# Windowed attention and two MLPs on one core: first six attention rounds on PSUM banks of their own and ahead of the weight conversions

## The chip, the core and the metric

The kernel runs on one core of a Trainium2 chip. Times are device microseconds of that core: the median of several runs, and beside it one execution that the hardware profiler recorded. TensorE (PE in the profile) multiplies matrices, VectorE (DVE), ScalarE (ACT) and GpSimd (POOL) work elementwise, SyncE (SP) issues the transfers. Each engine works through its own queue in order; semaphores tie the queues together.

## The reference, cut to what matters

```
scores = scale * q @ k.T                # 4 batches, 8 heads, 576 x 64 each
mask:  heads 0-3: 0 <= i - j < 32       # "plain"
       heads 4-7: 0 <= i - j < 128 and (i - j) % 4 == 0   # "dilated"
attn = softmax(masked scores);  x = attn @ v      # -> x: 2304 x 512
h = x @ w_in;  g = max(0.01 * h, h);  x2 = g @ w_out       # 512 -> 2048 -> 512
a = x2 @ w1;  b = x2 @ w2;  out = (a * b @ w3) @ w_out2    # 512 -> 1024 -> 512
```

The weights come as float64.

## The kernel before

**Attention** is done in 32 rounds. A round is one pair of heads and either the first 320 or the last 256 tokens of a batch. For round n: `scores(n)` (L316) multiplies qT and kT into a PSUM bank, VectorE adds the mask (L336) and takes the maximum (L338), ScalarE does the exponential (L341); `normalize(n)` (L346) makes the reciprocal on VectorE and multiplies on GpSimd (L354); `transpose_p(n)` (L360) turns the probabilities on TensorE into two PSUM tiles `ps_p` of up to three blocks each (L370), which ScalarE copies to `pT` (L372); `values(n)` (L375) multiplies them with v into `ps_o`, ScalarE writes the high part of the tile `x` (L419) and VectorE the low part (L421). `transpose_qk(m)` (L288) turns q and k of a pair of heads on TensorE (L306), and VectorE copies them to qT and kT (L309, L311). All these PSUM tiles come from one pair of banks, tag "side"; there are two more pairs, tag "h" (`bank`) and tag "acc" (`bank2`, two tiles of two banks each).

**The MLPs** run with float32 split in a high and a low part, three matmuls for each product (`mm3`, L110, lines L112 to L114). The first MLP takes a run of tokens c (320 or 256) and goes through blocks f of 128 hidden columns: `hidden(c, f)` makes `ps_h`, ScalarE applies the slope (L472), VectorE and GpSimd split it into `gs`, and two blocks later `project` adds it to `ps_x`. Run c = 0 goes through blocks 0 to 7 first, then c = 1 through all 16, then c = 0 through 8 to 15, then the others.

**Weights.** Before a block f can be used, a block of w_in and one of w_out must be converted from float64: 32 jobs, numbered by pairs (job 2f is w_in, 2f+1 is w_out). Each is a load of 512 KB into a buffer `raw` (mostly one of eight in the pool `woB`), a scaling on GpSimd (L103), two ScalarE instructions into `r` (L143, L145), a shift (L146) and a join (L147) on VectorE, called shift and join below, and then the split: a high cast (L107) and a low part (L108), on engines that the letters in `MLP_CONV` name. One letter triple stands for a job in turn: the scaling's engine, the high cast's, the low part's (A ScalarE, D VectorE, G GpSimd).

**Order.** The start is written out as a string (L700): digits load q and k, a to d load v, F loads a weight, X starts rounds 0 and 1, A is two of the four steps of an attention round, C is one conversion. Twelve A are the first six rounds. After the string the loop over blocks does, for each block ("turn"), the hidden part, some conversions (`owed_w`), some attention steps (`pace`) and the lagged projection. A scheduler then places the instructions of each engine: what stands ahead in the program has precedence, what stands behind may fill gaps. SP's own order is kept as written while weights are still converted.

Of the kernel before, what the change touches and what calls it, by code (L numbers as in the profile page):

```python
# [28 lines left out]
def tile_window_attention_two_mlps(  # L29
# [17 lines left out]
    T, DM = out.shape  # L47
# [17 lines left out]
    HP = H // 2  # L65
# [19 lines left out]
    def bank2(name):  # L85
        return psum.tile([P, 2, 512], F32, tag="acc", name=name, bufs=2)

    def side_bank(name):
        return psum.tile([P, 512], F32, tag="side", name=name, bufs=2)
# [59 lines left out]

    engine_of = {"A": nc.scalar, "D": nc.vector, "G": nc.gpsimd}  # L150
    FOLD_CONV = ("GAD", "GAG")
    MLP_CONV = ("GAD", "GDD", "GAD", "GDG")
    LAST_CONV = ("GAD",)

    class Convert:
# [70 lines left out]
    def pair(pi):  # L226
        b, h0 = divmod(pi, HP)
        return b, 2 * h0, 2 * h0 < H // 2

    def load_qk(m):  # L230
        if m >= 2 * NPAIR:
            return
        pi, nm = seq[m // 2], "qk"[m % 2]
        b, h0, plain = pair(pi)
        c = 6 if plain else 8
        n = S // c
        if m < 2 * HP:
            t = win_p.tile([P, 8, 2, D], F32, tag="win", name=f"{nm}{pi}", bufs=NF)
        else:
            t = att.tile([P, 8, 2, D], F32, tag="nat", name=f"{nm}{pi}", bufs=2)  # L240
        src = q if nm == "q" else k
        o = (b * H + h0) * S * D
        for j in range(2):
            nc.sync.dma_start(
                t[:n, :c, j, :], rows(src, o + j * S * D, [[c * D, n], [D, c], [1, D]])
            )
        nat_t[nm, pi] = t
# [40 lines left out]
    def transpose_qk(m):  # L288

        if m >= 2 * NPAIR:  # L290
            return
        pi, nm = seq[m // 2], "qk"[m % 2]
        plain = pair(pi)[2]
        c = 6 if plain else 8
        n = S // c
        t = nat_t.pop((nm, pi))
        dst = att.tile([P, S], F32, tag=nm + "T", name=f"{nm}T{pi}", bufs=2)
        if plain:
            to = dst.rearrange("d (p g c) -> d g c p", g=2, p=n)
        else:  # L300
            to = dst.rearrange("d (c p g) -> d g c p", g=2, p=n)
        for g in range(2):
            ps = side_bank(f"ps_{nm}T{pi}_{g}")
            for c1 in range(c // 2):
                src = t[:n, g * (c // 2) + c1].rearrange("p j d -> p (j d)")
                nc.tensor.transpose(ps[:, c1 * n : (c1 + 1) * n], src, ident[:n, :n])  # L306
            src = ps[:, : S // 2].rearrange("d (c p) -> d c p", p=n)
            if nm == "q":
                nc.vector.tensor_scalar(to[:, g], src, SCALE, None, op0=ALU.mult)  # L309
            else:  # L310
                nc.vector.tensor_copy(to[:, g], src)  # L311
        qk_t[nm, pi] = dst
# [47 lines left out]
    def transpose_p(n):  # L360
        s, _ = sm.pop(n)
        nb = s.shape[1]
        t = att.tile([KB, NQ, P], F32, tag="pT", name=f"pT{n}", bufs=2)[:, :nb]
        groups = [(i0, min(i0 + GROUP, nb)) for i0 in range(0, nb, GROUP)]
        pss = []
        for g, (i0, i1) in enumerate(groups):
            ps = side_bank(f"ps_p{n}_{g}")
            pss.append(ps[:KB, : (i1 - i0) * P].rearrange("k (i p) -> k i p", p=P))
            for i in range(i0, i1):
                nc.tensor.transpose(pss[g][:, i - i0], s[:, i], ident)  # L370
        for ps, (i0, i1) in zip(pss, groups):
            nc.scalar.copy(t[:, i0:i1], ps)  # L372
        pt[n] = t
# [51 lines left out]
    N_EARLY = 6  # L425
# [213 lines left out]
    with ExitStack():  # L639
# [44 lines left out]
        def kr(prefix):  # L684
            return lambda i: rawp.tile([P, 512], I32, tag="kr", name=f"{prefix}{i}", bufs=KR)

        jobs = []
        for f in range(NF):
# [4 lines left out]
            )  # L693
        conv = Convert(jobs, raw_early, kr("w"), kr("r"), MLP_CONV)

        with tc.manual_schedule(engines={mybir.EngineType.SP}):


            first = attention(0, N_EARLY)
            for x in "0aM1bFF2cFF3dFFXACAACACAACACAACACAACAC":  # L700
                if x in "0123":
                    load_qk(2 * int(x))
                    load_qk(2 * int(x) + 1)
                elif x in "abcd":
                    load_v("abcd".index(x))
                elif x == "M":
                    build_masks()
                elif x == "X":
                    transpose_qk(0)
                    transpose_qk(1)  # L710
                    scores(0)
                    scores(1)
                    transpose_qk(2)
                    normalize(0)
                    transpose_qk(3)
                elif x == "A":
                    step(first, first)
                elif x == "F":
                    conv.fetch()
                else:  # L720
                    conv.step()
            step(*[first] * 10)
# [6 lines left out]
        def mlp1(c, f, f0, f1):  # L729
            hidden(c, f)  # L730
            todo.append((c, f, f0, f1))

        def lagged():
            if len(todo) > LAG:
                project(*todo.pop(0))
# [18 lines left out]
        owed, owed_w = [0.0], [0.0]  # L754

        def pace(c):

            if xs_b[0] is None:
                owed[0] += 1.25 if turn < 8 else 0.25
            else:  # L760
                owed[0] += 2 if c < 2 else 1.5
            while owed[0] >= 1:
                owed[0] -= 1
                step(stream)
# [3 lines left out]
        turn = -1  # L768
        sp = ExitStack()
        for c, f0, f1 in runs:  # L770
# [38 lines left out]
            for f in range(f0, f1):  # L809
                turn += 1  # L810
                sp.close()
                if xs_b[0] is None:
                    sp.enter_context(tc.manual_schedule(engines={mybir.EngineType.SP}))
                mlp1(c, f, f0, f1)
                if xs_b[0] is None:
                    owed_w[0] += 1.5
                    while owed_w[0] >= 1:
                        owed_w[0] -= 1
                        conv.step()
                    if conv.made == len(conv.jobs) and not conv.done:  # L820
                        raw_es.close()
                        xsB_es, xs_b[0] = pool("xsB", "left")
                if c < C_LATE:
                    pace(c)
                elif c < NCH - 1:
                    fold_step()
                lagged()
                if c == NCH - 1:
                    conv.step()
                    if 2 <= f < 2 + NI:  # L830
                        load_wp(f - 2)
                    if 3 <= f < 3 + NI:
                        split_wp(f - 3)
                    if 11 <= f < 11 + NC:
                        split_y(0, f - 11)
                    if f == 11 + NC - 1:
                        load_y(1)
# [54 lines left out]
```

## Time and profile before

| | |
|---|---|
| median of 3 runs | 933.92 us (929.98 to 934.81) |
| profiled execution | 930.62 us, span 928.8 us |
| TensorE busy | 882.4 us, 95% of the span |
| VectorE, ScalarE, GpSimd busy | 352.9, 347.4, 250.6 us |
| TensorE's share of the chain that ended last | 81%, VectorE 9% |

In the 40 slices of the page TensorE is at nine tenths or more from the sixth slice on; the first five read 5, 6, 5, 7, 8. VectorE reads 4, 8, 9, 9, 9, 5 in the first six. The busy time of an engine is a share of a stretch: an engine that is full in one stage and half idle in the next shows as little in the sum as one that is never full. So the profile is read here by stretches, and then by what each engine waited for.

### The profile page before, as it was taken

The page shows a single profiled execution, that of the slowest core. Times are in us where ns is not written, and L with a number is a line of the kernel's source. Part 1 is how long each engine was busy: PE and PEld are TensorE (multiplying, and loading weights), DVE is VectorE, ACT ScalarE, POOL GpSimd, SP SyncE. Part 2 cuts the span into 40 slices and gives each one's busy share as a digit, 9 for nine tenths or more (in the row PEclk, how much of TensorE's full clock was granted, in tenths as well). Part 3 has the DMA queues.
Part 4 walks back from the last instruction along what each step waited for, and adds up shares of the span by engine and source line. Part 5 has one row for each costly group of instructions (what it writes and reads, how often), then busy time and mean ns, then how long its engine had stood idle before and what let it go on. Part 6 is the DMA issues. An engine that isn't in the chain of part 4 may idle for free.

```text
span 928.8 us, 16028 instructions
## 1 busy us (share of the span) xinstructions
PE 882.4 (95%) x6456; PEld 831.5 (90%) x6456; DVE 352.9 (38%) x715; ACT 347.4 (37%) x888; POOL 250.6 (27%) x288
## 2 busy tenths in 40 slices
PE   5657899999999999999999999999999999999998
PEld 4436899999999999999999999999999998999997
DVE  4899954443323323245333326871101010100000
ACT  3777633333333333455333225751312121211111
POOL 3365310002222222246221224432303131211110
PEclk9999999999999999999999999999999999999999
DMA  7993410332122211149688664630101010000000
GB/s 177 316 283 104 133 48 16 75 88 71 27 65 72 48 28 50 59 150 332 205 289 281 222 201 156 205 114 1 46 23 35 33 36 24 12 23 12 12 23 35
DMA packets 110938, 95.94 MB, mean 103 GB/s; under 512 B 69520, under 2 KB 94352, under 8 KB 110864
## 3 DMA queue, kind: packets, MB, share of 16 engines
q1 hardware_dynamic: 110864, 94.92, 33.6%
q8 instruction: 51, 0.84, 0.4%
q14 instruction: 23, 0.19, 0.1%
HBM read 78.51 MB, written 16.38 MB: 102 GB/s over the span
## 4 chain that ended last, share of the span: by engine, by line
PE 81%; DVE 9%; issue 3%; DMA 3%; ACT 2%; SPq 2%; POOL 1%; DVEq 0%; ACTq 0%; POOLq 0%
PE ps_ab L112 7%; PE ps_ab L114 7%; PE ps_ab L113 7%; PE ps_x L112 6%; PE ps_x L114 6%; PE ps_x L113 6%; PE ps_h L114 6%; PE ps_h L113 6%; PE ps_h L112 6%; PE ps_y L113 4%; PE ps_y L112 4%; PE ps_y L114 4%; PE ps_s L328 2%; PE ps_o L388 2%; PE ps_wp L114 2%
## 5 line engine op out<-in xcount | busy, mean ns | idle before, releaser
L112 PE MATMUL ps_h<-x,win 128*128 128x320 f32 (+1 forms) x512 | 153.8, 302 | 2.5 <-ACT x L419 1.4
L113 PE MATMUL ps_h<-x,win 128*128 128x320 f32 (+1 forms) x512 | 154.8, 302 | 1.1 <-DVE x L421 1.1
L113 PE MATMUL ps_x<-gs,wout 128*128 128x320 f32 (+1 forms) x512 | 152.7, 299 | 2.7 <-DVE gs L108 2.7
L114 PE MATMUL ps_h<-x,win 128*128 128x320 f32 (+1 forms) x512 | 154.3, 301 | 0.0
L112 PE MATMUL ps_x<-gs,wout 128*128 128x320 f32 (+1 forms) x512 | 152.6, 299 | 0.7 <-DVE x L508 0.7
L114 PE MATMUL ps_x<-gs,wout 128*128 128x320 f32 (+1 forms) x512 | 152.4, 298 | 0.0
L112 PE MATMUL ps_ab<-ys,w 128*128 128x384 f32 x384 | 130.1, 339 | 0.0
L114 PE MATMUL ps_ab<-ys,w 128*128 128x384 f32 x384 | 130.0, 339 | 0.0
L113 PE MATMUL ps_ab<-ys,w 128*128 128x384 f32 x384 | 130.0, 338 | 0.0
L615 DVE TENSOR_TENSOR ab<-a,ps_ab 128x384 f32<-128x384 f32 x48 | 26.6, 554 | 253.0 <-ACT a L613 247.9
L108 POOL TENSOR_TENSOR gs<-g,gs 128x320 fp32r<-128x320 f32 (+1 forms) x80 | 66.8, 837 | 164.9 <-DVE gs L107 154.2
L107 DVE CAST gs<-g 128x320 fp32r<-128x320 f32 (+1 forms) x128 | 48.8, 383 | 155.9 <-ACT g L472 155.4
L108 POOL TENSOR_TENSOR p<-ab,p 128x384 fp32r<-128x384 f32 x48 | 48.5, 1011 | 218.6 <-ACT p L107 218.6
L112 PEld LDWEIGHTS ps_h<-x,win 128*128 128x128 f32 x512 | 97.5, 191 | 3.5 <-ACT x L419 1.5
L113 PEld LDWEIGHTS ps_x<-gs,wout 128*128 128x128 f32 x512 | 96.9, 189 | 4.1 <-DVE gs L108 3.2
L113 PEld LDWEIGHTS ps_h<-x,win 128*128 128x128 f32 x512 | 97.7, 191 | 1.9 <-DVE x L421 1.5
L112 PEld LDWEIGHTS ps_x<-gs,wout 128*128 128x128 f32 x512 | 96.7, 189 | 2.2 <-DVE x L508 1.0
L114 PEld LDWEIGHTS ps_h<-x,win 128*128 128x128 f32 x512 | 97.7, 191 | 0.5
L472 ACT ACTIVATE g<-ps_h 128x320 f32<-128x320 f32 (+1 forms) x128 | 51.6, 403 | 122.6 <-PE ps_h L114 116.8
L114 PEld LDWEIGHTS ps_x<-gs,wout 128*128 128x128 f32 x512 | 96.9, 189 | 0.6
L613 ACT COPY a<-ps_ab 128x384 f32<-128x384 f32 x48 | 23.1, 481 | 143.9 <-PE ps_ab L114 143.9
L112 PEld LDWEIGHTS ps_ab<-ys,w 128*128 128x128 f32 x384 | 72.0, 188 | 1.2
(91 smaller groups left out, 1521.2 us busy)
## 6 DMA issues: line engine op xcount, KB each, us to landing
wo<-wo_dram SPq DMA_DIRECT2D x32, 512.0 KB
raw<-in_moe_w_in_dram SPq DMA_DIRECT2D x16, 512.0 KB
raw<-in_moe_w_out_dram SPq DMA_DIRECT2D x16, 512.0 KB
rawf<-in_moe_w_dram SPq DMA_DIRECT2D x16, 512.0 KB
raww<-in_moe_w_dram SPq DMA_DIRECT2D x16, 512.0 KB
v<-in_v_dram SPq DMA_DIRECT2D x60, 96.0 KB
q<-in_q_dram SPq DMA_DIRECT2D x32, 144.0 KB
k<-in_k_dram SPq DMA_DIRECT2D x32, 144.0 KB
```

The lines of the kernel that those rows point to most:

```text
L107: copy_on(e_hi)(hi, src)
L108: e_lo.tensor_tensor(lo, src, hi.bitcast(F32), op=ALU.subtract)
L112: nc.tensor.matmul(ps, a[1], b[0], start=first, stop=False)
L113: nc.tensor.matmul(ps, a[0], b[1], start=False, stop=False)
L114: nc.tensor.matmul(ps, a[0], b[0], start=False, stop=last)
L328: nc.tensor.matmul(ps[j * QB : (j + 1) * QB, i - bl.start], qt[d, i * QB : (i + 1) * QB], kt[d, first_key(i, plain) : first_key(i, plain) ...
L388: nc.tensor.matmul(ps[j * D : (j + 1) * D, i * QB : (i + 1) * QB], vt[i][:, h + j, :], t[:, i, j * QB : (j + 1) * QB], start=True, stop=True,)
L472: nc.scalar.activation(g, ps, AF.Prelu, alpha=SLOPE)
L613: nc.scalar.copy(t, ps[0][:, :TB])
L615: nc.vector.tensor_tensor(g, t, ps[1][:, :TB], op=ALU.mult)
```

## The change

Five edits, all of which act on the first part of the program:

- the string has eight F ahead of X instead of six, and all twelve A ahead of all eight C;
- in rounds 0 to 5 the two `ps_p` tiles lie in one tile of two banks of tag "acc"; the transposes of the first eight q and k tiles go to the banks of tag "h";
- the high casts of all w_out blocks are on ScalarE (half of all high casts; VectorE had them); the engines of the low parts stay;
- a turn has 1.75 conversions instead of 1.5;
- from turn 8 to the end of the conversions a turn has no attention step instead of 0.25.

```diff
-    MLP_CONV = ("GAD", "GDD", "GAD", "GDG")
+    MLP_CONV = ("GAD", "GAD", "GAD", "GAG")
...
-            ps = side_bank(f"ps_{nm}T{pi}_{g}")
+            ps = (bank if m < 2 * HP else side_bank)(f"ps_{nm}T{pi}_{g}")
...
+        both = bank2(f"ps_p{n}") if n < N_EARLY else None
         for g, (i0, i1) in enumerate(groups):
-            ps = side_bank(f"ps_p{n}_{g}")
+            ps = both[:, g] if both is not None else side_bank(f"ps_p{n}_{g}")
...
-            for x in "0aM1bFF2cFF3dFFXACAACACAACACAACACAACAC":
+            for x in "0aM1bFF2cFF3dFFFFXAAAAAAAAAAAACCCCCCCC":
...
-                owed[0] += 1.25 if turn < 8 else 0.25
+                owed[0] += 1.25 if turn < 8 else 0
...
-                    owed_w[0] += 1.5
+                    owed_w[0] += 1.75
```

VectorE's queue from the kT copies of the fourth head pair to the masked scores that follow them; `w`, `win` and `wout` are weights, `s` scores, `x` attention output. Before:

```order
L311 COPY kT_549<-ps_kT_0_550 128x3x96
L147 ISA w_734<-w_734,r_735 128x1024
L146 TENSOR_SCALAR w_767<-w_767 128x512
L311 COPY kT_549<-ps_kT_1_555 128x3x96
L147 ISA w_767<-w_767,r_768 128x1024
L108 TENSOR_TENSOR win_776<-w_734,win_776 128x512
L146 TENSOR_SCALAR w_865<-w_865 128x512
L107 CAST wout_874<-w_767 128x512
L146 TENSOR_SCALAR w_877<-w_877 128x512
L147 ISA w_865<-w_865,r_866 128x1024
L108 TENSOR_TENSOR wout_874<-w_767,wout_874 128x512
L336 TENSOR_TENSOR s_583<-ps_s_572,masks 128x480
```

And now, on the same engine and at the same place of the program:

```order
L311 COPY kT_504<-ps_kT_0_505 128x3x96
L311 COPY kT_504<-ps_kT_1_510 128x3x96
L350 TENSOR_SCALAR total_459<-total_459 128x5
L146 TENSOR_SCALAR w_684<-w_684 128x512
L422 TENSOR_TENSOR x_3_487<-ps_o_476,x_3_487 128x2x144
L422 TENSOR_TENSOR x_3_487<-ps_o_476,x_3_487 128x32
L353 RECIPROCAL rec_501<-total_459 128x5
L147 ISA w_684<-w_684,r_685 128x1024
L146 TENSOR_SCALAR w_696<-w_696 128x512
L147 ISA w_696<-w_696,r_697 128x1024
L336 TENSOR_TENSOR s_526<-ps_s_515,masks 128x480
```

The two copies now stand side by side, and four instead of nine weight instructions stand ahead of the scores.

TensorE's queue around round 2's values; `ps_p` are transposed probabilities, `ps_s` scores, `ps_qT` and `ps_kT` transposed q and k, `ps_o` values. Before:

```order
L370 MATMUL ps_p_1_467<-ident,s_337 96x128 x2
L328 MATMUL ps_s_476<-kT_426,qT_356 64x96 x10
L306 MATMUL ps_qT_0_498<-ident,q_202 128x96 x3
L306 MATMUL ps_qT_1_503<-ident,q_202 128x96 x3
L388 MATMUL ps_o_508<-pT_462,v_0_102 64x64 x8
L388 MATMUL ps_o_508<-pT_462,v_4_103 64x64 x2
L370 MATMUL ps_p_0_537<-ident,s_405 96x128 x3
L370 MATMUL ps_p_1_541<-ident,s_405 96x128
```

And now:

```order
L371 MATMUL ps_p_432<-ident,s_340 96x128 x5
L389 MATMUL ps_o_418<-pT_377,v_0_175 64x64 x8
L328 MATMUL ps_s_444<-kT_407,qT_350 64x96 x10
L306 MATMUL ps_qT_0_466<-ident,q_202 128x96 x3
L306 MATMUL ps_qT_1_471<-ident,q_202 128x96 x3
L371 MATMUL ps_p_493<-ident,s_398 96x128 x4
L389 MATMUL ps_o_476<-pT_431,v_0_102 64x64 x8
L389 MATMUL ps_o_476<-pT_431,v_4_103 64x64 x2
```

The transposes of a round are now one piece in one tile, and those of round 3 (`s_398`) stand ahead of round 2's values (`pT_431`).

ScalarE's queue in front of the high part of the fourth tile of x. Before:

```order
L107 CAST win_1159<-w_1138 128x512
L143 ACTIVATE r_1212<-raw_938 128x512
L145 ACTIVATE r_1212<-raw_938 128x512
L341 ACTIVATE s_699,total_703<-s_699,nmax_701 128x96 x4
L419 CAST x_1_719<-ps_o_708 128x320
```

And now:

```order
L107 CAST wout_872<-w_851 128x512
L143 ACTIVATE r_918<-raw_679 128x512
L145 ACTIVATE r_918<-raw_679 128x512
L107 CAST win_926<-w_863 128x512
L420 CAST x_1_636<-ps_o_625 128x320
```

A high cast of w_out now stands there, and the conversions are earlier ones: job 11 (`raw_679`) instead of job 18 (`raw_938`).

## Rows read from the trace of the kernel before

**Rows 1.** Stretches: us; length; busy PE, PEld, DVE, ACT, POOL (count); clock; DMA; GB/s
```profile
20.00:40.00 20.00, 14.17 (x118) 10.26 (x119) 15.50 (x33) 14.12 (x42) 7.33 (x9) 1.00 1.09 283
40.00:60.00 20.00, 9.73 (x84) 6.71 (x85) 19.46 (x39) 17.16 (x43) 12.46 (x11) 1.00 0.95 276
60.00:78.40 18.40, 10.43 (x89) 7.82 (x85) 18.27 (x34) 15.80 (x43) 9.91 (x10) 1.00 0.67 236
0.00:78.40 78.40, 43.60 (x356) 32.57 (x356) 62.10 (x125) 53.13 (x146) 37.37 (x56) 1.00 0.85 241
78.40:120.40 42.00, 36.61 (x289) 34.12 (x290) 41.19 (x78) 27.14 (x63) 17.48 (x19) 1.00 0.41 114
120.40:928.80 808.40, 802.24 (x5813) 764.85 (x5811) 249.59 (x514) 267.10 (x680) 195.79 (x214) 1.00 0.29 89
```

**Rows 2.** Timeline of TensorE: start, us, line, tiles, count, [idle before <- releaser]
```profile
5.33 1.19 PE L306 MATMUL ps_qT<-ident,q 72*128 72x72 f32 x8 [5.33 <-DMA q<-in_q_dram]
...
24.82 1.34 PE L388 MATMUL ps_o<-pT,v 96*64 96x64 f32 x20 [0.42 <-DVE qT L309]
...
40.64 1.33 PE L388 MATMUL ps_o<-pT,v 96*64 96x64 f32 x20 [0.17 <-DVE qT L309]
...
51.75 1.86 PE L328 MATMUL ps_s<-kT,qT 64*64 64x96 f32 x20 [3.74 <-DVE kT L311]
...
70.60 1.33 PE L388 MATMUL ps_o<-pT,v 96*64 96x64 f32 x20
...
78.93 0.63 PE L113 MATMUL ps_h<-x,win 128*128 128x320 f32 x1 [1.09 <-DVE x L421]
79.36 0.47 PE L114 MATMUL ps_h<-x,win 128*128 128x320 f32 x1
79.63 0.47 PE L112 MATMUL ps_h<-x,win 128*128 128x320 f32 x1
...
82.80 0.31 PE L114 MATMUL ps_h<-x,win 128*128 128x320 f32 x1
82.95 0.31 PE L112 MATMUL ps_h<-x,win 128*128 128x320 f32 x1
...
87.80 0.42 PE L113 MATMUL ps_x<-gs,wout 128*128 128x320 f32 x1 [1.44 <-DVE gs L108]
```

**Rows 3.** Timeline of VectorE: the second kT copy, and the low part x1
```profile
51.02 0.67 DVE L311 COPY kT<-ps_kT 128x288 f32<-128x288 f32 x1
...
78.40 0.48 DVE L421 TENSOR_TENSOR x<-ps_o,x 128x320 fp32r<-128x320 f32 x1
```

**Rows 4.** Groups by line and shape, 0 to 125 us: busy, mean ns, idle before
```profile
L147 DVE CUSTOM_DVE_ANT_0 w<-w,r 128x1024 uint16<-128x1024 uint16 x32 | 25.4, 800 | 1.8 <-ACT r L145 1.7
L143 ACT ACTIVATE r<-raw 128x512 f16<-128x512 f32 x32 | 25.2, 787 | 13.2 <-DVE win L108 4.8 <-DMA raw<-in_moe_w_in_dram 2.7 <-DVE wout L108 1.7
L145 ACT ACTIVATE r<-raw 128x512 int16<-128x512 uint32 x32 | 24.3, 761 | 0.0
L146 DVE TENSOR_SCALAR w<-w 128x512 int32<-128x512 int32 x32 | 18.9, 594 | 3.9 <-POOL w L103 3.8
L108 DVE TENSOR_TENSOR win<-w,win 128x512 fp32r<-128x512 f32 x16 | 12.3, 767 | 0.0
L107 ACT CAST win<-w 128x512 fp32r<-128x512 f32 x16 | 9.8, 611 | 4.3 <-DVE w L147 4.3
L107 DVE CAST wout<-w 128x512 fp32r<-128x512 f32 x16 | 9.3, 581 | 0.1
L108 DVE TENSOR_TENSOR wout<-w,wout 128x512 fp32r<-128x512 f32 x8 | 5.9, 736 | 0.0
```

**Rows 5.** Timeline of ScalarE: the cast of x0
```profile
62.99 0.39 ACT L419 CAST x<-ps_o 128x320 fp32r<-128x320 f32 x1
```

**Rows 6.** SP's issue of q for round 8, and the slowest load in the chain
```profile
45.42 1.71 SPq L244 DMA_DIRECT2D q<-in_q_dram  x2
41.94 9.29 DMA raw<-in_moe_w_in_dram
```

## The prediction

> **What bounds the kernel now.** I read the stretch view first, because it separates stages with different limits. From 120.4 us to the end TensorE is busy 802.24 of 808.40 us [rows 1]: that part is TensorE's own work, 6.2 us of idle time is all that could be won there, and the change removes no matmul. Ahead of it TensorE is busy 43.60 of 78.4 us, then 36.61 of 42.0 us. So 34.8 + 5.4 = 40.2 of its 46.4 idle us lie in the ramp, and the prediction is about the ramp alone.
>
> What holds TensorE there? VectorE is busy 15.50 of 20 us in 20 to 40, then 19.46 of 20 and 18.27 of 18.4 [rows 1]: from 40 us on it is full. ScalarE is second (17.16 and 15.80). The rows on TensorE show how that reaches it. The value matmuls of rounds 0 and 2 stand at 24.82 and 40.64, those of round 5 at 70.60: 7.9 us per round first, 10.0 us after. One wait is plain: scores that wait 3.74 us for kT [rows 2]. VectorE's rows give the reason: the second of the two kT copies starts at 51.02 [rows 3], and between it and the first the order of before (above) has two instructions that convert weights. The milestone is **x1**, VectorE's low part of the fourth head-pair tile, at 78.40 [rows 3]. Block 0 of the first MLP cannot finish without it; behind it matmuls follow at 0.27 us, from 82.80 on at 0.15 us [rows 2].
>
> **The change, part by part.** By count the engines run the same instructions, except that 16 high casts of w_out go from VectorE to ScalarE. Everything else is order.
>
> *VectorE ahead of x1.* In the program order 124 instructions stand ahead of it before, 96 after. What goes behind it: 9 casts at 0.581, 3 low parts of w_in at 0.767, 2 of w_out at 0.736, 7 shifts at 0.594 and 7 joins at 0.800 [rows 4]; a half of a later qT that also goes and a reciprocal that comes are left out. That is 5.23 + 2.30 + 1.47 + 4.16 + 5.60 = 18.8 us. These durations overlap a little in the queue, so 18.8 is the upper end. The lower is 28 times the mean of all 125 instructions up to 78.4, 62.10 / 125 = 0.497 us [rows 1]: 13.9 us. The instructions that move are longer than that mean, so I take the middle, 16.4 us. With VectorE full from 40 us on, x1 moves from 78.4 to 62.0. With less queued, some new idle time must appear on VectorE; it has 0.54 + 0.13 us in 40 to 60 and 60 to 78.4, and 4.5 in 20 to 40 [rows 1], so between 0 and 4.5; I take 1.0, since the converted blocks still fill most gaps. x1: 63.0, a gain of 15.4 us.
>
> *The casts.* ScalarE needs 0.611 us for a cast of this size, VectorE 0.581 [rows 4], so the move itself saves nothing on an engine sum; it pays because VectorE is the full one. Five of them stand ahead of x1 on ScalarE (one shows in the order above), but 7 pairs of conversions (0.787 + 0.761) and 3 casts of w_in go behind: 3.1 - 10.8 - 1.8 = -9.6 us [rows 4]. So ScalarE's queue ahead of x1 gets shorter too.
> The Trainium skill (ScalarE: Activation LUTs, Rules for kernel authors) speaks against this part: simple elementwise work belongs on VectorE. By it the nine casts would be worth nothing, the 16.4 us would shrink by their share of 5.23 / 18.8 to 11.8, and the time would be 4.6 us above my forecast. The rows say a full VectorE counts more than 0.03 us a cast; I follow them.
>
> *PSUM banks.* Probabilities get two banks per round, the q/k transposes the banks of block outputs that are unused so far; scores and values keep the side pair. This removes waits of the kind "a transpose waits until an eviction frees a bank". It gives TensorE up to 34.8 us of waits to lose, but TensorE's floor for x1 is far below: first matmul at 5.33 plus 43.60 busy, about 49 us [rows 1, 2]. So banks don't set the time, VectorE does, and I count them at nothing beyond making 62.0 reachable. If they did nothing, see the second rival.
>
> *Loads.* The first eight weight loads keep their places on SP's queue; two of them merely wait for no conversion. The load of q for round 8's pair stands behind 18 weight loads instead of 17, and the last of these needs the buffer of job 8 (before: job 7). SP issued that q at 45.42 [rows 6]. Job 8's ScalarE readers now stand just ahead of the cast of x0 (the third tile, values of round 4), which ran at 62.99 [rows 5]; if that gains as much as x1 it runs at 47.6, if only ScalarE's own 9.6 us, at 53.4. A load issued then may take as long as the 9.29 us of the slowest one in the chain [rows 6], so it lands between 57 and 63, at the latest with x1. I count 0; if it is later, TensorE waits, since the transposes of this q stand in its queue behind the first products with x1.
>
> *Behind x1.* From x1 to the high cast of the last block output of the first run, VectorE has 64 instructions ahead instead of 72: eight casts, 8 x 0.581 = 4.6 us less. TensorE could use up to its idle 5.4 us, but VectorE was not the only one that held it and ScalarE receives those casts; between 0 and 4.6 I take 1.4, nearer the lower end, because TensorE was already 87% busy there [rows 1].
>
> *Pace.* Conversions at 1.75 instead of 1.5 a turn and no attention step in the turns up to the end of the conversions: all of it behind 120 us, where TensorE is full. The rounds stand some ten matmuls earlier in its order than before. Its cover is TensorE's own work; without it at most the 6.2 us are at stake in either direction. I count 0.
>
> **Sum.** 15.4 + 1.4 = 16.8 us off the profiled execution's 930.62 us (span 928.8 plus 1.8 around it): 913.8. The three runs of before stand at 929.98, 933.92 and 934.81, so the profiled one is near the lower end and the median 3.3 above it. I set the forecast 1.2 above the sum: 915.
>
> **The rivals.**
> *ScalarE becomes the bound.* It was idle for 5.9 + 2.8 + 2.6 = 11.3 us of the 58.4 from 20 us to x1 [rows 1]. If it keeps all of that idle time, because its in-order queue holds conversions ahead of the probability copies, x1 moves only by its own 9.6 us, to 68.8: 921.0, or 922 on the forecast's scale. For: 47.1 - 9.6 = 37.5 us of its work would be left for the 43 us from 20 to 63. Against: those 37.5 us fit.
>
> *Rounds are held by their own latency.* If the pitch of the first three rounds, 7.9 us at a time when VectorE was only 78% busy, is the best there is, the values of round 5 come at 24.82 + 5 x 7.9 = 64.3 instead of 70.6, and the gain is 6.3: 924 to 926. This is the case where the banks don't do what they are for.
>
> *Slower: the array stays at its low rate.* The 0.27 us spacing up to 82.6 and 0.15 us after are a factor of two, 1.2 against 2.4 GHz, though the granted clock reads 1.00 in all stretches [rows 1, 2]. The rise came after TensorE had run without a wait since 78.93. If blocks now come in short bursts, because the block outputs wait behind conversions on ScalarE and VectorE, each of the eight blocks of the first run costs 24 matmuls x 0.12 = 2.9 us more; from six blocks on (17.3 us) the gain is gone, and with eight the time is 930.62 - 16.8 + 23.0 = 937. Against: after the rise a wait of 1.44 us did not lower the rate [rows 2].
> The Trainium skill (TensorE: Matmul & The Clock Gate, Part 1) has it that idleness throttles the array again; no run here shows a fall after 82.8.
>
> **How the numbers follow.** Forecast (x1 between 58 and 67 us, 909 to 920): 0.70. ScalarE: 0.12. Latency: 0.08. No visible change, by a late q or several small losses: 0.05. Slower: 0.05. The range 908 to 925 holds the forecast, the ScalarE case and most of the latency case; its lower end takes both upper ends, 930.62 - 18.8 - 4.6 + 1.2 = 908.4. About 0.5%, 4.7 us, is what a measurement of this kernel can tell from no change. Faster by more than that: 0.70 + 0.12 + most of 0.08 = 0.88; within: 0.07; slower: 0.05.
>
> **What would show it.** Right: x1 near 63 us; kT copies side by side on VectorE; a round pitch of 6 to 7 us; TensorE's last projection of the first run near 103 instead of 120 us; the stretch behind it as long as before, 808 us within 2. Wrong: ScalarE over 95% busy between 20 and 60 with x1 near 69 (first rival); VectorE with several us of idle time in 40 to 60 at a pitch near 8 (second); 0.27 us spacing beyond 70 us (third); TensorE waiting on the load of q; or more than 3 us of new idle time behind the ramp.

## The result, and the profile after

The changed kernel takes **917.83 us** (median of 4 runs, 916.27 to 918.36) against 932.91 us (929.98 to 934.81) for the kernel before on the same chip: a ratio of 0.9838, 95% interval 0.9808 to 0.9869. It is faster by 1.6%, 15.1 us between the medians. The profiled execution takes 918.02 us with a span of 916.2 us, 12.6 us less than the profiled one of before. The difference between 15.1 and 12.6 is what the prediction said of the profiled execution of before: it lay 2 to 3 us under its own median. Forecast was 915.

The page first: engines (busy, share of the span, instructions), then VectorE's busy tenths and TensorE's granted clock in 40 slices.

```profile
PE 880.8 (96%) x6456; PEld 832.4 (91%) x6456; DVE 345.9 (38%) x699; ACT 354.5 (39%) x904; POOL 247.8 (27%) x288
...
DVE  4999864444333233264334345851101010100000
...
PEclk9559999999999999999999999999999999999999
```

The sixteen casts stand in the counts (VectorE 715 to 699, ScalarE 888 to 904). The clock row says nothing of the kernel before, whose row is all nines; more of that at the end. The stretches of after (columns as in [rows 1]):

```profile
20.00:40.00 20.00, 15.02 (x133) 11.68 (x135) 17.10 (x36) 17.00 (x56) 7.64 (x8) 0.58 1.05 277
40.00:60.00 20.00, 12.10 (x122) 9.54 (x118) 18.38 (x38) 19.73 (x56) 10.41 (x12) 0.59 1.01 289
0.00:62.08 62.08, 39.01 (x352) 31.21 (x352) 46.06 (x96) 44.14 (x133) 27.21 (x48) 0.69 0.91 242
100.00:110.00 10.00, 6.74 (x66) 5.53 (x65) 8.69 (x18) 9.24 (x23) 4.85 (x5) 0.93 0.69 222
103.36:916.20 812.84, 804.44 (x5816) 766.38 (x5814) 260.55 (x531) 278.29 (x701) 202.75 (x222) 1.00 0.30 91
```

Up to x1 VectorE ran 96 instructions in 46.06 us instead of 125 in 62.10 [rows 1]. But from 40 to 60 us the full engine is now ScalarE (19.73 of 20), no longer VectorE (18.38). And there is a stretch that the kernel before does not have: from 100 to 110 us TensorE is busy for only 6.74 us.

VectorE after, which answers [rows 3]: the second kT copy of the fourth pair (before at 51.02), x1 (before at 78.40), and the low part of round 7's tile, the last that the second run of blocks (c = 1) needs:

```profile
38.70 0.68 DVE L311 COPY kT<-ps_kT 128x288 f32<-128x288 f32 x1 [0.30 <-PE ps_kT L306]
...
62.08 0.48 DVE L422 TENSOR_TENSOR x<-ps_o,x 128x320 fp32r<-128x320 f32 x1
...
107.85 0.41 DVE L422 TENSOR_TENSOR x<-ps_o,x 128x256 fp32r<-128x256 f32 x1
```

TensorE after, which answers [rows 2]: the values of rounds 0, 2 and 5, the first matmuls that read the high part of the fourth tile, the end of the low rate, and then the hand-over from the first run of blocks to the second:

```profile
23.18 0.80 PE L389 MATMUL ps_o<-pT,v 96*64 96x64 f32 x12 [0.16 <-ACT pT L373]
...
35.15 1.34 PE L389 MATMUL ps_o<-pT,v 96*64 96x64 f32 x20
...
56.92 0.90 PE L389 MATMUL ps_o<-pT,v 96*64 96x64 f32 x20 [2.64 <-ACT pT L373]
60.15 0.90 PE L112 MATMUL ps_h<-x,win 128*128 128x320 f32 x2 [2.33 <-DMA v<-in_v_dram]
...
67.08 0.47 PE L113 MATMUL ps_h<-x,win 128*128 128x320 f32 x1
67.35 0.47 PE L114 MATMUL ps_h<-x,win 128*128 128x320 f32 x1
...
68.93 0.31 PE L114 MATMUL ps_h<-x,win 128*128 128x320 f32 x1
69.08 0.31 PE L112 MATMUL ps_h<-x,win 128*128 128x320 f32 x1
...
104.24 0.31 PE L114 MATMUL ps_x<-gs,wout 128*128 128x320 f32 x1
105.72 0.50 PE L112 MATMUL ps_h<-x,win 128*128 128x256 f32 x2 [1.16 <-ACT x L420]
106.72 0.42 PE L371 MATMUL ps_p<-ident,s 128*96 128x128 f32 x2 [0.50 <-ACT pT L373]
108.31 1.55 PE L328 MATMUL ps_s<-kT,qT 64*64 64x96 f32 x20 [1.17 <-DVE x L422]
...
110.59 0.41 PE L113 MATMUL ps_h<-x,win 128*128 128x256 f32 x1
110.80 0.41 PE L114 MATMUL ps_h<-x,win 128*128 128x256 f32 x1
...
112.45 0.28 PE L112 MATMUL ps_h<-x,win 128*128 128x256 f32 x1
112.57 0.28 PE L113 MATMUL ps_h<-x,win 128*128 128x256 f32 x1
```

The first run's last projection ends at 104.5; after it TensorE waits three times within 4 us, and then its matmuls of 256 columns start 0.21 us apart instead of 0.12 until 112.1. In the clock's column (one slice of 3.4 us below) that is a granted clock of 0.50, the lower of the two levels:

```profile
108.70:112.10 3.40, 3.40 (x27) 3.18 (x24) 3.27 (x6) 3.23 (x7) 1.29 (x1) 0.50 0.89 236
```

What kept round 7's tile? Its values ran on TensorE at 100.95. ScalarE's rows show its high part (L420) behind four casts of weights, VectorE's low part comes another 2.2 us later. The first row is the cast of x0, which answers [rows 5], the second that of the fourth tile (x1's high part); SP's issue of q for round 8 answers [rows 6]:

```profile
50.53 0.43 ACT L420 CAST x<-ps_o 128x320 fp32r<-128x320 f32 x1
...
59.64 0.46 ACT L420 CAST x<-ps_o 128x320 fp32r<-128x320 f32 x1
...
103.21 0.62 ACT L107 CAST win<-w 128x512 fp32r<-128x512 f32 x1 [0.76 <-DVE w L147]
103.74 1.65 ACT L107 CAST wout<-w 128x512 fp32r<-128x512 f32 x3
105.30 0.36 ACT L420 CAST x<-ps_o 128x256 fp32r<-128x256 f32 x1
```
```profile
50.66 1.71 SPq L244 DMA_DIRECT2D q<-in_q_dram  x2
```

To see where the gain stands at each point of the program, I counted the matmuls of the first MLP (lines L112 to L114 on `ps_h` and `ps_x`) in TensorE's timeline and read when the same number starts; eight blocks of the first run are 192 of them. The rows merge neighbours, so a time is good to about 0.1 us; and near the hand-over the matmuls of two runs are mixed, so number 192 marks an amount of work and not the last projection of the first run.

| matmul of the first MLP | 1 | 12 (needs x1) | 96 | 192 | 240 | 288 | 400 | 800 | span |
|---|---|---|---|---|---|---|---|---|---|
| before, us | 63.44 | 79.89 | 99.05 | 120.17 | 128.63 | 134.36 | 150.29 | 222.63 | 928.8 |
| after, us | 51.02 | 63.58 | 82.46 | 103.36 | 116.08 | 123.44 | 139.62 | 210.92 | 916.2 |
| gain, us | 12.4 | 16.3 | 16.6 | 16.8 | 12.6 | 10.9 | 10.7 | 11.7 | 12.6 |

16.8 us were won when the first run's worth of matmuls was done, the very sum of the prediction. About 6 us of it were lost again within the next 20 us, and 2 came back later.

### The profile page after: what moved, and what is told of

It is laid out like the page before. It is cut to its first block, busy times and chain, and to the rows that moved or that the text cites. A ratio compares the mean times of both kernels' runs of the same rounds, so it can differ in the third digit from the quotient of the medians.

```text
span 916.2 us, 16026 instructions
## 1 busy us (share of the span) xinstructions
PE 880.8 (96%) x6456; PEld 832.4 (91%) x6456; DVE 345.9 (38%) x699; ACT 354.5 (39%) x904; POOL 247.8 (27%) x288
## 4 chain that ended last, share of the span: by engine, by line
PE 82%; DVE 6%; ACT 3%; DMA 3%; SPq 2%; issue 2%; POOL 1%; DVEq 0%; POOLq 0%; ACTq 0%
PE ps_ab L112 7%; PE ps_ab L114 7%; PE ps_ab L113 7%; PE ps_h L113 6%; PE ps_h L114 6%; PE ps_x L112 6%; PE ps_h L112 6%; PE ps_x L114 6%; PE ps_x L113 6%; PE ps_y L113 4%; PE ps_y L112 4%; PE ps_y L114 4%; PE ps_s L328 2%; PE ps_o L389 2%; PE ps_wp L114 2%
## 5 line engine op out<-in xcount | busy, mean ns | idle before, releaser
L112 PE MATMUL ps_h<-x,win 128*128 128x320 f32 (+1 forms) x512 | 154.7, 303 | 3.6 <-DMA v<-in_v_dram 2.3
L114 PE MATMUL ps_h<-x,win 128*128 128x320 f32 (+1 forms) x512 | 154.4, 302 | 0.0
L112 PE MATMUL ps_x<-gs,wout 128*128 128x320 f32 (+1 forms) x512 | 152.1, 299 | 1.1 <-DVE x L509 1.1
L114 PE MATMUL ps_x<-gs,wout 128*128 128x320 f32 (+1 forms) x512 | 152.7, 299 | 0.0
L112 PE MATMUL ps_ab<-ys,w 128*128 128x384 f32 x384 | 130.1, 339 | 0.0
L114 PE MATMUL ps_ab<-ys,w 128*128 128x384 f32 x384 | 130.0, 339 | 0.0
L112 PEld LDWEIGHTS ps_h<-x,win 128*128 128x128 f32 x512 | 97.9, 192 | 5.3 <-ACT x L420 4.2
L112 PEld LDWEIGHTS ps_x<-gs,wout 128*128 128x128 f32 x512 | 96.5, 189 | 2.6 <-DVE x L509 1.3
L114 PEld LDWEIGHTS ps_h<-x,win 128*128 128x128 f32 x512 | 98.4, 192 | 0.3
L114 PEld LDWEIGHTS ps_x<-gs,wout 128*128 128x128 f32 x512 | 96.9, 189 | 0.5
L473 ACT ACTIVATE g<-ps_h 128x320 f32<-128x320 f32 (+1 forms) x128 | 51.4, 403 | 115.2 <-PE ps_h L114 114.1
L112 PEld LDWEIGHTS ps_ab<-ys,w 128*128 128x128 f32 x384 | 72.0, 188 | 1.2
```

The source lines that it names most:

```text
L112: nc.tensor.matmul(ps, a[1], b[0], start=first, stop=False)
L114: nc.tensor.matmul(ps, a[0], b[0], start=False, stop=last)
L473: nc.scalar.activation(g, ps, AF.Prelu, alpha=SLOPE)
```

## The experiments

Two questions: which of the five edits made the gain, and what took the 6 us back at the hand-over? My theory for the second, after the first four runs (called **H** below): the second run needs attention rounds that stand in TensorE's queue behind the first run and that depend on VectorE and ScalarE, which are still converting weights. If the first run ends earlier, TensorE only reaches these steps earlier and waits. The first rival: the converted blocks themselves are late. All kernels were timed beside the kernel before, whose median was 931.98 to 932.91 us. "Matmul 192" and "288" are read as above; "last join" is the end of the last of the 32 joins on VectorE, that is the end of the conversions.

| kernel | median of its runs, us | ratio (95%) | x1 | matmul 192 | matmul 288 | last join |
|---|---|---|---|---|---|---|
| before | 932.91 | 1 | 78.40 | 120.17 | 134.36 | 114.5 |
| **changed** | 917.83 | 0.9838 (0.9808 to 0.9869) | 62.08 | 103.36 | 123.44 | 119.6 |
| before + both bank edits | 923.14 | 0.9899 (0.9884 to 0.9914) | 57.91 | 99.2 | 126.6 | 116.9 |
| changed, no bank edit | 930.21 | 0.9972 (0.9959 to 0.9985) | 80.38 | 118.4 | 131.4 | 117.0 |
| changed, q/k banks undone | 919.13 | 0.9857 (0.9833 to 0.9881) | 64.03 | 101.5 | 122.5 | 118.6 |
| changed, p banks undone | 921.55 | 0.9885 (0.9863 to 0.9907) | 70.25 | 109.9 | 124.6 | 116.1 |
| before + casts on ScalarE | 931.58 | 0.9997 (0.9985 to 1.0008) | 80.29 | 120.2 | 134.4 | 112.7 |
| changed, casts on VectorE | 924.63 | 0.9917 (0.9902 to 0.9932) | 58.38 | 96.0 | 127.6 | 121.9 |
| changed, 1.5 a turn | 915.80 | 0.9823 (0.9803 to 0.9844) | 61.32 | 102.0 | 119.9 | 118.0 |
| changed, ten blocks | 914.85 | 0.9810 (0.9795 to 0.9825) | 60.76 | 102.2 | 118.5 | 116.4 |
| changed, casts on VectorE, ten blocks | 915.28 | 0.9818 (0.9803 to 0.9833) | 58.62 | 95.8 | 118.6 | 123.2 |
| changed, twelve blocks | 913.84 | 0.9802 (0.9785 to 0.9818) | 60.89 | 102.4 | 118.6 | 116.6 |
| before, ten blocks | 932.12 | 0.9997 (0.9987 to 1.0006) | 78.97 | 121.0 | 135.7 | 115.3 |
| changed, 1.5 a turn, twelve blocks | 911.67 | 0.9777 (0.9753 to 0.9801) | 60.60 | 96.8 | 117.0 | 115.6 |

### The banks, alone and left out

The kernel before with the two bank edits and nothing else:

```diff
-            ps = side_bank(f"ps_{nm}T{pi}_{g}")
+            ps = (bank if m < 2 * HP else side_bank)(f"ps_{nm}T{pi}_{g}")
...
+        both = bank2(f"ps_p{n}") if n < N_EARLY else None
...
-            ps = side_bank(f"ps_p{n}_{g}")
+            ps = both[:, g] if both is not None else side_bank(f"ps_p{n}_{g}")
```

> The kernel before with the PSUM banks alone (its own start string, casts and rates). In its queue VectorE has 97 instructions and 11 joins ahead of x1, where before has 124 and 19. Theory A (x1 is set by what stands ahead of it on VectorE, and it is the banks that let the attention stand there): x1 at 62 to 66 us, time 917 to 921. Rival B (the written order does it, the banks only save short eviction waits): x1 not ahead of 75 us, time 929 to 934.

Measured 923.14 us. Rival B falls, and theory A's ranges are missed on both sides: the banks alone bring x1 to 57.91, 4 us earlier than all five edits together, and matmul 192 to 99.2. At the end only 9.2 us are left. Its stretches, the second one inside the first run, and TensorE at the hand-over:

```profile
40.00:60.00 20.00, 12.74 (x98) 10.10 (x97) 20.00 (x41) 18.27 (x52) 11.05 (x11) 0.50 0.90 259
87.90:91.30 3.40, 3.40 (x25) 2.98 (x25) 3.40 (x9) 2.00 (x7) 1.04 (x1) 0.50 0.38 87
100.00:110.00 10.00, 5.04 (x47) 3.64 (x47) 9.93 (x20) 8.46 (x21) 5.54 (x5) 0.75 0.78 244
```
```profile
104.07 0.69 PE L389 MATMUL ps_o<-pT,v 96*64 96x64 f32 x16 [2.52 <-DVE kT L311]
...
108.83 1.86 PE L328 MATMUL ps_s<-kT,qT 64*64 64x96 f32 x20 [1.59 <-DVE x L422]
```

From 100 to 110 us TensorE is busy for half the time, VectorE for all of it: the first run ended early and the attention steps of rounds 6 to 8 wait for VectorE. From 105 to 115.2 the granted clock is 0.50, as it already was for 3.4 us inside the first run, behind a wait of 1.86 us.

The counterpart, the changed kernel with the old lines for the banks:

```diff
-            ps = (bank if m < 2 * HP else side_bank)(f"ps_{nm}T{pi}_{g}")
+            ps = side_bank(f"ps_{nm}T{pi}_{g}")
...
-        both = bank2(f"ps_p{n}") if n < N_EARLY else None
+        both = None
```

> The changed kernel with all PSUM tiles of the attention back on the side pair; string, casts and rates of the change stay. VectorE has 119 instructions and 20 joins ahead of x1. Theory A: x1 at 74 to 78 us, time 926 to 933. Rival B (the written order does it): x1 at 63 to 66 us, time 918 to 921.

Measured 930.21 us, in theory A's range, with x1 at 80.38, later than its 74 to 78. Without the banks the other four edits are worth 0.3%. In the program's order x1 is then the 120th instruction of VectorE (with all edits the 97th, before the 125th): where the steps are written in the string does not decide what stands first, whether their PSUM tile is free does. So the order that carried the prediction's sum is the work of the bank edits.

### Each bank edit alone

The probabilities keep their banks, the q/k transposes go back to the side pair:

```diff
-            ps = (bank if m < 2 * HP else side_bank)(f"ps_{nm}T{pi}_{g}")
+            ps = side_bank(f"ps_{nm}T{pi}_{g}")
```

> The changed kernel with the q/k transposes back on the side pair; only the probabilities of rounds 0 to 5 keep banks of their own. In VectorE's program order x1 then has 102 instructions ahead of it (all banks: 97, none: 120, which ran at 62.1 and 80.4 us, 0.80 us each). Theory B (the banks act through VectorE's order): x1 at 65 to 68, the end of the first run 3 to 5 us later than in the changed kernel. Since the changed kernel waits about 6 us at the hand-over for round 7's tile, which stands behind the same 27 joins in both, theory H adds that most of this delay is absorbed there: 917 to 920. Without that absorption it is passed on: 921 to 923.

Then the reverse, only the q/k transposes keep theirs:

```diff
-        both = bank2(f"ps_p{n}") if n < N_EARLY else None
+        both = None
```

> The changed kernel with the probabilities back on the side pair; only the q/k transposes keep the other banks. 109 instructions of VectorE ahead of x1 (all banks 97, none 120). Theory B: x1 at 70 to 73, the first run ends at 111 to 113; theory H: nothing is left to absorb it, round 7's tile then stands behind 29 joins instead of 27: 922 to 926. If instead either bank edit alone frees the side pair enough: x1 within 2 us of 62.1 and 916 to 919.

Measured 919.13 us with x1 at 64.03, and 921.55 us with x1 at 70.25. Among these kernels, which all have the casts on ScalarE, x1 follows its place in VectorE's order (97th, 102nd, 109th, 120th: 62.1, 64.0, 70.3, 80.4 us), so theory B holds for x1. It does not hold for the end of the first run in the first kernel: that was to come 3 to 5 us later, and matmul 192 comes 1.9 us earlier (101.5). So this kernel, whose 1.3 us the intervals do not tell from nothing, says nothing of absorption. The second does: matmul 192 is 6.5 us later than in the changed kernel, the time 3.7, which is the absorption that H expects. But H in its narrow form, that round 7's tile is what TensorE waits for, falls with the first of these kernels. VectorE's row of that tile, and TensorE's waits behind it:

```profile
102.02 0.42 DVE L422 TENSOR_TENSOR x<-ps_o,x 128x256 fp32r<-128x256 f32 x1
```
```profile
106.84 0.47 PE L306 MATMUL ps_qT<-ident,q 96*128 96x96 f32 x3 [0.68 <-ACT pT L373]
109.18 0.47 PE L306 MATMUL ps_qT<-ident,q 96*128 96x96 f32 x3 [1.87 <-DVE s L336]
111.43 1.29 PE L389 MATMUL ps_o<-pT,v 96*64 96x64 f32 x20 [1.78 <-DVE qT L309]
```

The tile is there 5.8 us earlier than in the changed kernel, and matmul 288 comes only 1 us earlier: TensorE goes on to the next attention steps in its queue and waits 4.3 us for those. It is not one tile that is late but the whole chain of attention steps, whose VectorE parts are queued among the last conversions.

### The casts

The changed kernel with the high casts of w_out on VectorE again:

```diff
-    MLP_CONV = ("GAD", "GAD", "GAD", "GAG")
+    MLP_CONV = ("GAD", "GDD", "GAD", "GDG")
```

> The changed kernel with the high casts of w_out back on VectorE. Theory A of the prediction (a quarter of what leaves VectorE ahead of x1 is casts, 4.6 us): x1 at 66 to 68 us, 921 to 923. Rival C (the scheduler fills the same gaps with fewer conversions instead, 11 joins ahead of x1): x1 within 1.5 us of 62.1, time 916 to 920. Rival D (on ScalarE the casts hold up round 7 at the end of the first run): x1 as in C, but the wait of about 5 us near 105 us shrinks, 912 to 916.

Measured 924.63 us, above the ranges of A, C and D. x1 is neither later nor the same but 3.7 us earlier (58.38), matmul 192 even 7 us earlier (96.0), and that with VectorE busy for all of 40 to 60 us. Ahead of x1 the order with the casts on ScalarE cost time; 2.0 us of it lie in joins that GpSimd held up (last section). The stretch from 40 to 60, and then the two in which the clock is low and TensorE's waits ahead of the first of them:

```profile
40.00:60.00 20.00, 12.78 (x106) 10.04 (x103) 20.00 (x40) 18.46 (x53) 11.52 (x12) 0.50 0.95 293
...
101.75:112.00 10.25, 9.19 (x63) 7.84 (x64) 9.57 (x18) 8.61 (x22) 5.14 (x5) 0.50 0.76 229
118.85:122.25 3.40, 3.40 (x17) 3.40 (x18) 3.40 (x12) 1.56 (x4) 1.64 (x1) 0.50 0.02 5
```
```profile
101.74 0.74 PE L306 MATMUL ps_kT<-ident,k 72*128 72x72 f32 x4 [3.29 <-DVE s L336]
...
116.12 0.50 PE L112 MATMUL ps_x<-gs,wout 128*128 128x256 f32 x2 [1.99 <-DVE gs L107]
118.10 0.68 PE L389 MATMUL ps_o<-pT,v 96*64 96x64 f32 x14 [1.48 <-DVE qT L309]
```

The first run is done earlier, so TensorE waits longer (3.29 us for VectorE's masked scores), and its clock then falls for 10.2 us and once more for 3.4. What that costs is an estimate from the spacing: 0.213 against 0.12 us for the same matmul, so 44% of TensorE's busy time there: 0.44 x (9.19 + 3.40) = 5.5 us, against 0.44 x 3.40 = 1.5 us in the changed kernel. 4.0 of the 6.8 us between the two kernels would be the clock. This is an upper estimate: part of that busy time is attention matmuls, whose spacing was not compared, and time lost where another wait follows costs nothing.

If the casts matter only at the hand-over, more blocks in the first run should hide them. The same kernel with a first run of ten blocks:

```diff
-        runs = [(0, 0, NF // 2), (1, 0, NF), (0, NF // 2, NF)]
+        runs = [(0, 0, 10), (1, 0, NF), (0, 10, NF)]
```

> The changed kernel with two edits: the high casts of w_out on VectorE as before, and a first run of ten blocks instead of eight. With eight blocks the casts on VectorE cost 6.8 us (924.63 against 917.83). Theory H: the casts on ScalarE pay only at the hand-over from the first run to the second, where VectorE's queue still held them; with ten blocks the wait for round 7's tile is covered, so this kernel comes within 2 us of the ten blocks with casts on ScalarE (914.85): 913 to 917, no low clock behind 100 us. Theory S: the casts on VectorE slow the supply of converted blocks anyway, and blocks 8 and 9 are asked for earlier now: TensorE waits for gs or wout in the first run instead, 919 to 923.

Measured 915.28 us: with ten blocks it makes no difference where the casts are (914.85). On the time theory H holds and S falls. H's reason holds only in part: the first run now ends at 109.8 us, and TensorE still waits 1.57, 0.57 and 1.31 us for attention steps between 107 and 115 us. It is busy for two thirds of the stretch, but here the clock stays up:

```profile
105.00:115.20 10.20, 6.76 (x62) 5.75 (x61) 10.16 (x19) 6.27 (x12) 4.60 (x5) 1.00 0.83 256
```

And the casts moved in the kernel before:

```diff
-    MLP_CONV = ("GAD", "GDD", "GAD", "GDG")
+    MLP_CONV = ("GAD", "GAD", "GAD", "GAG")
```

> The kernel before with the high casts of w_out on ScalarE and nothing else. The prediction counted a quarter of its gain, 4.6 us, to casts that leave VectorE ahead of x1. Theory Q: that holds whatever the order: x1 at 73 to 75 instead of 78.4, 926.5 to 928.5. Theory H: the casts only matter where the hand-over waits, and here it doesn't: x1 within 2.5 us of 78.4 or later, 930 to 934.

Measured 931.58 us, ratio 0.9997, x1 at 80.29: nothing, with x1 1.9 us later. Theory Q falls.

### The length of the first run

The changed kernel with the line for ten blocks above:

> The changed kernel with ten instead of eight blocks in the first run (0 to 9, the rest later), so that TensorE has two blocks, 7 us of matmuls, more to do before it needs round 7. Theory A (what was won up to the end of the first run and lost right after it, 16.8 against 10.6 us, was lost to the wait for round 7's tile and to the slower clock behind that wait): the lost 6 us come back, 910 to 914. Rival E (the wait is for VectorE's and ScalarE's backlog whatever TensorE does meanwhile, so it only moves by two blocks): 916 to 919.

Measured 914.85 us, between the two ranges: 3.0 us better than the change. Matmul 288 comes at 118.5 instead of 123.4, although 48 of the matmuls up to it now have 320 columns instead of 256 (0.15 against 0.12 us each). The stretch from 100 to 110 us, which now lies ahead of the first run's end at 114.6, and the longest wait in it:

```profile
100.00:110.00 10.00, 8.78 (x82) 8.30 (x79) 8.71 (x16) 8.48 (x17) 5.26 (x6) 1.00 0.60 200
```
```profile
107.37 1.04 PE L328 MATMUL ps_s<-kT,qT 64*64 64x96 f32 x20 [0.72 <-DVE x L422]
```

TensorE is busy 8.78 instead of 6.74 of 10 us, and the clock does not fall. With twelve blocks (`(0, 0, 12)` and `(0, 12, NF)`):

> The changed kernel with a first run of twelve blocks instead of eight (ten blocks gave 914.85). Theory H: the second run starts when round 7's tile is there (its low part at 106.9 to 108 us in every kernel with the banks); a first run that ends later than that waits for nothing at the hand-over: twelve blocks win another 1 to 2 us on ten, 912.5 to 914.5, matmul 288 of the MLP at 116 to 117.5 us. Theory S: by then the converted blocks are what is late; blocks 10 and 11 make TensorE wait within the first run, 915.5 to 919.

Measured 913.84 us, in H's range and 1 us better than ten, which the intervals do not tell apart. H's matmul 288 (116 to 117.5) was missed: it comes at 118.6, as with ten blocks. The control, ten blocks in the kernel before:

> Control: the kernel before with a first run of ten blocks and nothing else. Theory H: there the first run ends at 119.3 us, round 7's tile is there at 118.9, nothing waits at the hand-over and ten blocks change nothing: 930.5 to 934, the ratio within 0.3%. Theory G: the longer first run helps by itself, whatever the hand-over (fewer changes of run, conversions better covered): 3 us as on the changed kernel, 928 to 930.

Measured 932.12 us, 0.9997. There the first run ends when the attention steps are ready, and a longer one wins nothing. So the 3 us are won only where the banks made the first run early.

### The rate of conversions

```diff
-                    owed_w[0] += 1.75
+                    owed_w[0] += 1.5
```

> The changed kernel with 1.5 conversions a turn, as before, instead of 1.75. All queues come out as they do with the old string, so this undoes the string's longer F part and the rate at once. The prediction counted the rate at nothing. Theory N: within 1.5 us of the changed kernel, 916.5 to 919.5, x1 at 61 to 63. Theory R: fewer conversions per turn delay blocks 8 and on, the second run waits for them behind 125 us: 920 to 924, with waits of TensorE for win or wout there. If the conversions take less room at the hand-over, round 7 comes earlier: 914 to 916.

Measured 915.80 us, in the last of the three ranges, with round 7's tile at 105.11 instead of 107.85: 2 us better than the change in the median, with intervals that overlap. The rate is worth nothing that these runs can show, or a loss. The expectation lets this run stand for the string's edit too; no kernel with the old string and the other edits was run, so that is not shown. The pace of attention steps, the fifth edit, was not undone by itself either. What the runs show of these three is their sum. The changed kernel with the casts on VectorE is the banks, the string, the rate and the pace, and at 924.63 us it is no faster than the banks alone (923.14). The gain lies in the banks and, on top of them, in the casts. Nor does the loss at the hand-over come from the pace: the banks alone keep 0.25 steps a turn and lose more there. Both best edits together:

```diff
-        runs = [(0, 0, NF // 2), (1, 0, NF), (0, NF // 2, NF)]
+        runs = [(0, 0, 12), (1, 0, NF), (0, 12, NF)]
...
-                    owed_w[0] += 1.75
+                    owed_w[0] += 1.5
```

> The changed kernel with 1.5 conversions a turn and a first run of twelve blocks: the two edits that came out best, together. Theory H: round 7's tile came 2.7 us earlier with 1.5 conversions a turn (105.1), but with twelve blocks nothing waits for that tile any more, so the two gains (2.0 and 4.0 us) don't add: 912.5 to 915. If they are independent: 911 to 912.5. If blocks 8 to 11, whose conversion stands later in the order now, make the first run wait: 915 to 918.

Measured 911.67 us (910.41 to 913.57), ratio 0.9777: 6.2 us below the changed kernel, the sum of the two gains (2.0 and 4.0). By the medians they are independent, against what H said here; but the interval overlaps with that of twelve blocks alone, so this is not shown. One long wait is left, inside the first run, and behind it the granted clock is 0.50 from 100.1 to 103.5:

```profile
100.04 0.81 PE L371 MATMUL ps_p<-ident,s 128*96 128x128 f32 x3 [1.69 <-DVE total L350]
```

Why the slower rate may help was not followed further. This kernel is faster than the kernel before and the changed one.

## Why the prediction was right, and where it was not

**VectorE ahead of x1: right, almost to the number.** Predicted: 16.4 us less work, 1.0 us new idle, x1 at 63.0. Measured: VectorE's busy time up to x1 fell from 62.10 to 46.06, by 16.0 us; its idle time is 16.30 before and 16.02 after; x1 is at 62.08. The kT copies went ahead of the conversions (the second from 51.02 to 38.70), and the round pitch is (56.92 - 23.18) / 5 = 6.7 us. The first rows of the order foretold this.

**The casts: wrong.** A quarter of the gain was put down to nine casts that leave VectorE. Moved back, x1 is 3.7 us earlier; moved alone, nothing changes. The step that failed is "it pays because VectorE is the full one": with the banks VectorE is not the only full engine any more. ScalarE went from 17.16 to 19.73 of 20 us in 40 to 60, and TensorE waits 2.64 us for its probability copy ahead of round 5's values. So the first rival's engine, ScalarE, held x1 in part, though x1 came at 62 and not at its 68.8: the 37.5 us of work fitted, as the text said against it. How large its part is stays open, since 2.0 of the 3.7 us lie in joins that GpSimd held up. That the sum was right all the same is partly luck: the banks alone give 20.5 us at x1, more than the upper end of 18.8, and the casts take 4 back. The Trainium skill (ScalarE: Activation LUTs, Rules for kernel authors) puts relu, max, min, add and mul on VectorE; casts are not in that row, and the prediction read it as covering them. Read so, the runs agree with it ahead of x1 (58.38 against 62.08) and disagree on the whole, where the casts on VectorE cost 6.8 us; with a longer first run neither matters (914.85 and 915.28).

**PSUM banks: in the sum, but in a wrong place.** "Nothing beyond making 62.0 reachable" undersells them: the order of VectorE's queue, the largest term, follows from them, and without them x1 is at 80.4. The second rival (rounds held by their own latency) did not come: the pitch of the first rounds is 6.0 us, not 7.9.

**The load of q: right.** The cast of x0 ran at 50.53 (47.6 to 53.4 predicted), q was issued at 50.66, and TensorE never waits for it. The wait of 2.33 us that the row at 60.15 puts down to a load of v ends 0.05 us after ScalarE's cast of the tile that this matmul reads (59.64 + 0.46), so the cast is the likelier reason.

**Behind x1: mis-sized.** From x1 to matmul 192 the change won 0.5 us, not 1.4. The sign for it, the last projection of the first run "near 103 instead of 120 us", came at 104.5; but in the kernel before that projection ends at 124.8, not at 120.

**The stretch behind: this is the step that failed.** "808 us within 2" and "I count 0. Its cover is TensorE's own work". From matmul 192 on it was 928.8 - 120.17 = 808.6 us before and is 812.8 now, 4.2 us longer: 2.0 us more busy time (804.44 against 802.47) and 2.2 us more idle. I took the stretch behind 120 us as a property of the program, but it was one of the moment: TensorE was full there because VectorE had nearly finished the conversions. The change moves their end, from 114.5 to 119.6 us, while the first 192 matmuls are through 17 us earlier. The cover went, and what is late next, the chain of rounds 6 to 8, was not asked for. 16.3 + 0.5 - 4.2 = 12.6 us, the difference of the two profiled spans.

**The slower rival: its mechanism came, its price did not.** The array does fall back to the low rate, which no run before the prediction had shown. In the changed kernel it does so after the hand-over and not in the first run: for 3.4 us, at most about 1.5 us by the spacing, and at most about 5.5 us where the casts stay on VectorE. With the banks alone it also falls inside the first run, as the rival said, for 3.4 us from 87.9. Each of these falls follows a stretch in which TensorE waited. The Trainium skill (TensorE: Matmul & The Clock Gate, Part 1) has it that idleness throttles the array again; these falls agree with it. Not every wait brings a fall: with ten blocks and the casts on VectorE the clock stays at 1.00 with TensorE busy for 6.76 of 10.2 us.

What stays open: why 2 us come back between matmul 400 and the end, why 1.5 conversions a turn is not worse, and what the string and the pace are worth by themselves.

## What to carry to other kernels

Where a scheduler places work, ask which buffers it waits for before asking how the code is written: the two edits on PSUM banks by themselves took twenty-seven instructions from ahead of x1 (124 to 97), the other four edits without them five (119). When a stage is made earlier, find the next step in the waiting engine's queue and ask whether its other inputs get earlier too; if they don't, give the engine work that depends on nothing (here two to four more blocks) before it comes to that step. A move of work between two engines can help at one point and cost at another; its price is read at each of them.

## What the runs showed of the hardware

**The clock column is blank before its first event.** In the kernel before it reads 1.00 everywhere [rows 1], though the spacing up to 82.6 us is that of the low rate [rows 2]. The kernel before with ten blocks has the same ramp, the same work in it, and reads otherwise in these two stretches:

```profile
60.00:80.00 20.00, 10.96 (x95) 8.47 (x96) 19.88 (x36) 17.36 (x48) 10.46 (x11) 0.88 0.66 221
80.00:100.00 20.00, 19.27 (x146) 18.36 (x146) 20.00 (x38) 13.62 (x32) 8.39 (x10) 0.86 0.41 105
```

So a stretch ahead of the first recorded change of the clock must be judged by the matmuls' spacing.

**A VectorE instruction can stand still, within its recorded time, until a GpSimd instruction ends.** Up to 58 us a join takes 878 ns in the changed kernel and 700 ns with the casts on VectorE; the first of these groups is from the changed kernel, the second from the one with the casts on VectorE (columns as in [rows 4]):

```profile
L147 DVE CUSTOM_DVE_ANT_0 w<-w,r 128x1024 uint16<-128x1024 uint16 x11 | 9.7, 878 | 0.6 <-ACT r L145 0.4
```
```profile
L147 DVE CUSTOM_DVE_ANT_0 w<-w,r 128x1024 uint16<-128x1024 uint16 x11 | 7.7, 700 | 0.9 <-ACT r L145 0.7
```

That is 2.0 us over eleven joins. ScalarE, which has the casts, is not the reason. One of the long joins of the changed kernel, and the GpSimd instruction that was running when it began:

```profile
46.30 1.14 DVE L147 CUSTOM_DVE_ANT_0 w<-w,r 128x1024 uint16<-128x1024 uint16 x1
```
```profile
46.13 0.77 POOL L103 TENSOR_SCALAR w<-raw 128x512 f32<-128x512 f32 x1 [2.12 <-DVE wout L108]
```

The scaling ends at 46.90, the join 0.54 us later. The fourteen traces have 448 such joins. The 235 with no GpSimd instruction beside them take 671 to 704 ns. Of the 123 that begin while a GpSimd instruction has more than 0.13 us left to run, 112 end 0.54 to 0.55 us after it, and the longest takes 1793 ns. Four of the first eleven joins of the changed kernel are of this kind, and one of those of the other kernel. So where these joins fall is a matter of the order, and not a price of the casts. This is read from traces made for other questions; no run moved GpSimd's work to test it.
